# One row buffer for a two-pass channel-attention kernel: packed blocks read whole, other fills, fewer stores

## The chip, the core and the metric

The kernel runs on one core of a Trainium2 chip. The metric is the device time of one execution in microseconds (us). All tensors are bfloat16 in HBM; a "row" below means 768 bytes (384 channels) on each of the 128 partitions, 98,304 bytes in all.

## What is computed

The input `x` is 384 x 384 positions of 384 channels, 113.25 MB. Over all positions the mean and the maximum of each channel are taken, both go through the same small two-layer net, and a sigmoid gives one factor for each channel, by which the whole input is multiplied.

```python
xf = x.reshape(B, H * W, C)
gap = jnp.mean(xf, 1)
gmp = jnp.amax(xf, 1)
h_a = gap @ w1
h_a = h_a * (h_a > 0)
h_m = gmp @ w1
h_m = h_m * (h_m > 0)
scale = _sigmoid(h_a @ w2 + h_m @ w2)
return x * scale[:, None, None, :]
```

So every row must be read once before any row can be multiplied, and stored once after. What does not stay in the core's memory between the passes must be read a second time.

## The kernel before

The input is 1,152 rows, in blocks of some rows each (lines 112 to 123). A transfer moves n rows: on every partition one contiguous run of n x 768 bytes. All reads go on SP's queue, all stores on ACT's queue; both are first in, first out. The order of all instructions is written out by hand (`manual_schedule`, line 180), so each engine runs its work in the order in which the text issues it, and a read on SP's queue that waits for its buffer holds up all reads behind it.

**Memory.** `body` (line 149) has 264 rows: three slots of 31, 31 and 34 rows for reads that pass through, and from row 96 on seven homes of 24 rows. `held` (line 148) is another buffer of 21 rows. `acc` has 11 rows.

**First pass** (lines 220 to 386). A list `steps` of reads, tests, packs and one judgement is built and then issued. Each read is followed by its column sums on TensorE (`sums`, line 259) and its running maximum on VectorE (DVE) into `acc` (`maximum`, line 328, in pieces of at most 6 rows that alternate between the two halves of `acc`, `HALVES`). Some rows stay for the second pass:

- seven *packed blocks* of 32 rows. Three quarters (24 rows) are read into the block's home, the fourth ("part d", 8 rows) into one of two places in `held` (line 153). TensorE and ACT pack the 32 rows into the 24 of the home (`pack`, line 305), in two halves; ACT also tests whether the packing is without loss (`test`, line 295). The place of d is then free for the block after next.
- the last fills of the three slots (`STAYING`) and the last 21 rows, in `held` (`LAST_HELD`).
- ten rows copied into PSUM (line 383 and 385), and eight turned over into PSUM (`turn_over`, line 331) so that other rows can be refilled into their place (line 405).

Between the blocks, fills of up to 31 rows go round the three slots (`BETWEEN`, `PASSING`, `fill`, line 208). The last four reads are summed in another way (`tail_sums`, line 276), after the sums so far are turned (`turn_sums`, line 271). Before the last but one read's maxima `acc` is folded from 11 rows to 6 (`FOLD_BEFORE`, line 365).

**Between the passes** (lines 389 to 421). The two weight matrices are read, the refill of 8 rows and parts of `acc` as buffers are read, the maxima are folded, and the factors `scale_bc` come from ACT at line 421.

**Second pass** (lines 424 to 575). The rows that stayed are multiplied and stored, the 29 places of `PLACES` are read again (782 rows), multiplied and stored, and the packed blocks are unpacked in between (`unpack`, line 452), multiplied and stored by `finish` (line 484) and, for blocks 2 to 6, by the list `after` (line 500) in the last three turns. A place may be read as soon as its rows have left (`read`, line 509). At the end (line 576) stands a branch that reads the packed blocks again if a test failed; with this data it isn't taken.

Of the kernel before, what the change touches and what calls it, by code (L numbers as in the profile page):

```python
# [30 lines left out]
SLOT = 31  # L31
SLOTS = 3
RING = 96
G = 8
PACKED = 7
PSUM_ROWS = 8
# [3 lines left out]
HELD_ROWS = 21  # L40
# [4 lines left out]
FOLD_BEFORE = 2  # L45
BETWEEN = (
    (10, 31, 31, 31), (31, 31, 31), (31, 31, 31, 31), (31, 31, 31), (31, 31, 31, 31), (31, 31, 31), (30, 27),
)
PASSING = (25, 22, 21, 10, 17)
SHARED_FILL = 2  # L50
STAYING = {0: (16, 15), 1: (11, 10, 10), 2: (10, 9, 4, 6, 5)}
LAST_HELD = (6, 5, 4, 6)
# [7 lines left out]
FILLS = 16  # L60
# [5 lines left out]
HELD_STORES = (6, 7)  # L66
# [6 lines left out]
def kernel(  # L73
# [14 lines left out]
    NS = SLOTS  # L88
# [11 lines left out]
    consts = ctx.enter_context(tc.tile_pool(name="consts", bufs=1))  # L100
    xpool = ctx.enter_context(tc.tile_pool(name="xp", bufs=1))
# [511 lines left out]
```

## Time and profile before

| what | us |
|---|---|
| median of 3 runs | 728.07 (727.78 to 728.39) |
| the profiled execution, its own time | 727.18 |
| its span, first to last instruction | 725.4 |
| DVE busy in it | 565.1 |
| ACT busy in it | 349.6 |
| PE busy in it | 188.9 |

A profile is one execution. Its page shows busy times, the span in 40 slices of 18.1 us with the rate of the transfers in each, and the chain of waits that ended last. Views beside the page group busy time by stretches of the span, list instructions in order of time, list who waited for whom, and group instructions by their shape. Engines: PE = TensorE, PEld its weight loads, DVE = VectorE, ACT = ScalarE, SP = the queue of reads, ACTq = the queue of stores.

### The profile page before, as it was taken

How to read it: one execution, taken by the hardware profiler on the slowest of the kernel's cores; microseconds unless marked ns; L12 is line 12 of the kernel's file. 1: busy time of each engine (PE TensorE's matmuls, PEld its weight loads, DVE VectorE, ACT ScalarE, POOL GpSimd, SP SyncE). 2: the span in 40 equal slices, each digit the busy share in tenths (PEclk: the TensorE clock that was granted, in tenths of full speed). 3: DMA queues.
4: the chain of work that ended last, by engine and by line, in shares of the span. 5: the costliest groups of instructions: out<-in, count | busy, mean ns of one | idle time of the engine just before them, and what ended most of it. 6: DMA issues, size and time to landing. Idle time of an engine off the chain costs nothing.

```text
span 725.4 us, 3863 instructions
## 1 busy us (share of the span) xinstructions
PE 188.9 (26%) x1357; PEld 73.4 (10%) x1357; DVE 565.1 (78%) x438; ACT 349.6 (48%) x251; POOL 0.7 (0%) x6
## 2 busy tenths in 40 slices
PE   5756576876776561000000000000000000001000
PEld 1222222322222130000000000000000000001000
DVE  6899999989999998897966454798888889496200
ACT  6979999999999200057230022806254451200000
POOL 0000000000000000000000000000000000000000
PEclk9898977887988555555555555555555555555555
DMA  9999999999999988999999999999999999999998
GB/s 382 429 427 423 432 425 435 426 432 427 426 428 422 421 330 347 399 425 437 425 438 424 434 434 428 425 433 428 431 437 428 429 436 432 432 430 442 426 427 362
DMA packets 21843, 305.63 MB, mean 421 GB/s; under 512 B 2784, under 2 KB 3136, under 8 KB 8512
## 3 DMA queue, kind: packets, MB, share of 16 engines
q1 hardware_dynamic: 14048, 192.14, 62.4%
q10 hardware_dynamic: 7776, 113.25, 36.7%
q8 instruction: 10, 0.16, 0.1%
q14 instruction: 9, 0.07, 0.0%
HBM read 192.14 MB, written 113.25 MB: 421 GB/s over the span
## 4 chain that ended last, share of the span: by engine, by line
DMA 71%; DVE 20%; issue 2%; PE 0%; ACT 0%; SPq 0%; ACTq 0%; DVEq 0%
DMA body<-in_x_dram 52%; DMA out_dram<-body 19%; DVE acc L329 11%; DVE body L426 7%; DVE held L426 1%; DVE held L458 0%; DVE kept_ps L383 0%; DVE acc L426 0%; ACT held L477 0%; DVE acc L463 0%; DVE acc L370 0%; PE bank_a L263 0%; DVE body L458 0%; SPq L360 0%; PE bank_a L420 0%
## 5 line engine op out<-in xcount | busy, mean ns | idle before, releaser
L426 DVE TENSOR_TENSOR body<-body,scale_bc 128x9216 bf16<-128x9216 bf16 (+8 forms) x49 | 220.1, 4523 | 88.7 <-DMA body<-in_x_dram 87.5
L329 DVE TENSOR_TENSOR acc<-acc,body 128x2304 bf16<-128x2304 bf16 (+4 forms) x210 | 229.7, 1167 | 14.1 <-DMA body<-in_x_dram 14.1
L263 PE MATMUL bank_a<-body,small 128*1 128x512 bf16 (+2 forms) x849 | 91.8, 476 | 82.0 <-DMA body<-in_x_dram 82.0
L335 PE MATMUL words_ps<-ident_bf,acc 128*128 128x128 bf16 x24 | 2.7, 313 | 376.9 <-DVE acc L568 376.9
L291 ACT ACTIVATE held<-held 128x3072 uint8<-128x3072 uint8 (+1 forms) x35 | 82.0, 2344 | 1.1
L477 ACT COPY held<-body 128x1536 uint8<-128x1536 uint8 x8 | 11.8, 1474 | 141.6 <-DVE body L426 141.4
L290 ACT ACTIVATE held<-body,held 128x3072 uint8<-128x3072 int8 (+1 forms) x28 | 61.9, 2211 | 9.7 <-DMA body<-in_x_dram 9.2
L477 ACT COPY body<-body 128x1536 uint8<-128x1536 uint8 x20 | 29.5, 1476 | 63.3 <-DVE body L426 62.8
L477 ACT COPY body<-acc 128x1536 uint8<-128x1536 uint8 x34 | 49.5, 1473 | 8.0 <-DVE acc L463 7.6
L263 PEld LDWEIGHTS <-small 128*1 128x1 bf16 x891 | 30.2, 96 | 143.7 <-issue 123.3
L335 PEld LDWEIGHTS <-acc 128*128 128x128 bf16 x24 | 2.5, 147 | 377.3 <-DVE acc L568 377.3
L311 PE MATMUL words_ps<-body,scale_bc 128*128 128x512 fp8e4 (+1 forms) x126 | 39.6, 429 | 2.9 <-ACT body L318 2.9
L311 PE MATMUL words_ps<-body,w_sb 128*128 128x512 fp8e3 x84 | 27.1, 406 | 0.0
L311 PE MATMUL words_ps<-held,body 128*128 128x512 fp8e4 x84 | 25.5, 385 | 0.0
L317 ACT COPY body<-held 128x1536 uint8<-128x1536 uint8 x14 | 20.6, 1470 | 0.0
L477 ACT COPY acc<-body 128x1536 uint8<-128x1536 uint8 x14 | 20.5, 1466 | 0.0
L317 ACT COPY body<-body 128x1536 uint8<-128x1536 uint8 x14 | 20.4, 1461 | 0.0
L318 ACT ACTIVATE body<-words_ps 128x1536 uint16<-128x1536 f32 x14 | 20.1, 1439 | 0.0
L290 ACT ACTIVATE held<-held 128x3072 uint8<-128x3072 int8 x7 | 20.0, 2856 | 0.2
L329 DVE TENSOR_TENSOR acc<-acc,held 128x1920 bf16<-128x1920 bf16 (+4 forms) x18 | 17.5, 1012 | 0.1
L477 ACT COPY held<-acc 128x1536 uint8<-128x1536 uint8 x8 | 11.8, 1475 | 10.1 <-DVE acc L463 10.1
L458 DVE TENSOR_SCALAR held<-held 128x1536 uint16<-128x1536 uint16 x28 | 15.7, 560 | 1.0
(71 smaller groups left out, 173.4 us busy)
## 6 DMA issues: line engine op xcount, KB each, us to landing
body<-in_x_dram SPq DMA_DIRECT2D x20, 2976.0 KB, 21.7
body<-in_x_dram SPq DMA_DIRECT2D x16, 2880.0 KB, 25.0
out_dram<-body ACTq DMA_DIRECT2D x15, 2880.0 KB, 23.3
body<-in_x_dram SPq DMA_DIRECT2D x18, 2304.0 KB, 19.3
out_dram<-body ACTq DMA_DIRECT2D x16, 2304.0 KB, 21.8
out_dram<-body ACTq DMA_DIRECT2D x3, 4608.0 KB, 37.0
held<-in_x_dram SPq DMA_DIRECT2D x8, 768.0 KB, 22.4
body<-in_x_dram SPq DMA_DIRECT2D x5, 960.0 KB, 15.2
```

Source lines behind the costliest of these rows:

```text
L263: nc.tensor.matmul(sum_ps[q * QP:q * QP + 1, 0:g * P], lhsT=ones_bf[:, 0:1], rhs=rows[:, k:k + g, q * P:(q + 1) * P], start=(done + k == 0 ...
L290: nc.scalar.activation(out=out_, in_=rows, func=ACT.Square, bias=test_bias, scale=TEST_SCALE)
L291: nc.scalar.activation(out=out_, in_=out_, func=ACT.Square, bias=minus4, accum_out=tests[:, k:k + 1],)
L311: nc.tensor.matmul(words[:, c:c + BANK], lhsT=weights[2 * r + k], rhs=high(part(i, r), dt)[:, half * n + c:half * n + c + BANK], start=(r ...
L317: nc.scalar.copy(out=high(part(i, r), U8)[:, span], in_=low(part(i, r + 2), U8)[:, span])
L318: nc.scalar.activation(out=part(i, 2).rearrange("p n c -> p (n c)").bitcast(U16)[:, span], in_=words, func=ACT.Copy, bias=32767.5,)
L329: nc.vector.tensor_tensor(out=out_, in0=in0, in1=in1, op=ALU.max)
L335: nc.tensor.transpose(out=out_[:, r, q * P:(q + 1) * P], in_=rows[:, r, q * P:(q + 1) * P], identity=ident_bf)
L426: nc.vector.tensor_tensor(out=dst, in0=src, in1=scale_bc.unsqueeze(1).to_broadcast([P, n, C]), op=ALU.mult)
L458: nc.vector.tensor_scalar(out=u16(dst), in0=u16(src), scalar1=s1, scalar2=s2, op0=op0, op1=op1)
L477: nc.scalar.copy(out=dst, in_=src)
```

## The change

- `body` and `held` become one buffer `rows` of 285 rows: `held` is its first 5, `body` the 280 behind. The two places of d now lie inside `body` (`D_AT`), and the homes stand in another order (`HOME_AT`). In the source the rows of the packed blocks are ordered to fit (`FIRST_AT`, `FOURTH_AT`).
- Blocks 1, 2 and 3 are each read in one transfer of 32 rows, home and place of d together (`TOGETHER`). Blocks 0, 4, 5 and 6 are read in two parts as before (block 0 in three).
- Fills no longer go round three slots: each has its own place and size (`BETWEEN`, `PASSING` hold pairs of place and rows), and early ones also use homes that are not yet taken. The first has 21 rows where three reads of 8, 13 and 10 rows stood; the others between the blocks have 21 to 51.
- The second half of each packing is issued behind another fill (`PACK_BEHIND`); the judgement stands one slot later.
- The resident pieces of the slots are (16, 15), (11, 11, 9), (11, 10, 8, 5); the last four reads have 8, 2, 6 and 5 rows, and the eight rows that are turned over are the first of these.
- The packed blocks leave in five stores (two of 32 rows by `finish`, then 64, 48 and 48), where there were seven (48 and 16, then 48, 48, and 16, 24, 24). The ten rows kept in PSUM leave in one store instead of two, and the rows in `held` leave as 5 and 8.
- 24 instead of 16 small writes stand at DVE's start (`FILLS`).

```diff
@@ -28,28 +28,44 @@
-SLOT = 31
-SLOTS = 3
 RING = 96
 G = 8
 PACKED = 7
+HOME_AT = (96, 184, 128, 152, 256, 232, 208)
+D_AT = (120, 176)
+BODY_ROWS = 280
+FIRST_AT = (0, 104, 40, 64, 200, 176, 152)
+FOURTH_AT = (24, 96, 32, 88, 128, 136, 144)
+TOGETHER = (1, 2, 3)
+SLOTS = ((0, 31), (31, 31), (62, 34))
+SPARE = 93
 PSUM_ROWS = 8
 LATE_ROWS = 8
 BANK_ROWS = 2
 RING_BYTES = 256
-HELD_ROWS = 21
+HELD_ROWS = 5
 A = 11
 HALVES = ((0, 6), (6, 11))
 FIRST_LOAD = 4
 FOLD_BEFORE = 2
 BETWEEN = (
-    (10, 31, 31, 31), (31, 31, 31), (31, 31, 31, 31), (31, 31, 31), (31, 31, 31, 31), (31, 31, 31), (30, 27),
+    ((21, 30), (208, 48)), ((51, 21), (0, 49), (72, 21)), ((208, 51), (0, 46), (46, 34)),
+    ((208, 42), (0, 45), (45, 32)), ((208, 34), (0, 36), (36, 31), (67, 26)), ((0, 33), (33, 31), (64, 29)),
+    ((0, 25), (25, 23)),
 )
-PASSING = (25, 22, 21, 10, 17)
-SHARED_FILL = 2
-STAYING = {0: (16, 15), 1: (11, 10, 10), 2: (10, 9, 4, 6, 5)}
-LAST_HELD = (6, 5, 4, 6)
+PACK_BEHIND = (0, 2, 1, 1, 0, 0, 1)
+PASSING = ((62, 16), (78, 9), (0, 22), (31, 14), (45, 17))
+REFILL_AT = 62
+LAST_PASSING = (70, 17)
+STAYING = ((16, 15), (11, 11, 9), (11, 10, 8, 5))
+LAST_HELD = ((8,), (2, 6), (5,))
 PLACES = (
...
@@ -57,13 +73,12 @@
     + ((0, 30), (30, 30), (60, 30), (90, 30)) * 3 + ((0, 30), (30, 30), (60, 30), (90, 20))
 )
 FIRST_READ = (8, 16)
-FILLS = 16
+FILLS = 24
 OPENING = (0, 24, (3, 4))
 FIRST_PLACE = ((0, 8, (8, 8)), (0, 0, (8,)))
 SECOND_PLACE = ((1, 0, (8, 9)), (2, 0, (10,)))
 OTHER_PLACES = ((1, 17, (14,)), (2, 10, (24,)))
-HELD_STORES = (6, 7)
 TEST_SCALE = 0.031187
 SUM_TAIL = 4
 MM_ROWS = 4
...
@@ -109,16 +122,18 @@
         at += n
         return at - n, n
-    ps_block = take(PSUM_ROWS)
-    beside = take(BANK_ROWS + A)
+    for_psum = PSUM_ROWS + BANK_ROWS
+    first_block = take(for_psum + A)
     packed_block = take(GP * PACKED)
-    held_block = take(sum(LAST_HELD))
-    stay = {s: take(sum(pieces)) for s, pieces in STAYING.items()}
+    late_block, kept_block, held_block = (take(sum(pieces)) for pieces in LAST_HELD)
+    stay = [take(n) for _, n in SLOTS]
     refill = take(LATE_ROWS)
     passing_at, n_pass = at, TOT - at
-    between = [[take(n) for n in group] for group in BETWEEN]
-    passing = [take(n) for n in PASSING]
-    assert at == TOT and sum(n for _, n in PLACES) == n_pass and sum(LAST_HELD) == HELD_ROWS
+    between = [[take(n) for _, n in group] for group in BETWEEN]
+    passing = [take(n) for _, n in PASSING]
+    last_passing = take(LAST_PASSING[1])
+    assert at == TOT and sum(n for _, n in PLACES) == n_pass and held_block[1] == HELD_ROWS
+    assert late_block[1] == LATE_ROWS and kept_block[1] == G and [sum(p) for p in STAYING] == [n for _, n in SLOTS]
     at = passing_at
     again = [take(n) for _, n in PLACES]
...
@@ -145,14 +160,16 @@
     acc = consts.tile([P, A, C], BF16)
     nc.dynamic_dma_scratch_size = RING_BYTES
     nc.lookup_mloc("DynamicDMAScratchLoc").dims = [P, RING_BYTES]
-    held = nc.alloc_sbuf_tensor_at("held", [P, HELD_ROWS, C], BF16, offset=RING_BYTES).ap()
-    body = xpool.tile([P, RING + 3 * G * PACKED, C], BF16, name="body")
-    slots = [body[:, SLOT * i:SLOT * i + stay[i][1], :] for i in range(NS)]
-    spare = body[:, SLOT * NS, :]
-    homes = [body[:, RING + 3 * G * i:RING + 3 * G * (i + 1), :] for i in range(PACKED)]
-    fourth = [held[:, G * (i % 2):G * (i % 2 + 1), :] for i in range(PACKED)]
-    tested = held[:, 2 * G:2 * G + G // 2, :].rearrange("p n c -> p (n c)").bitcast(U8)
-    tests = held[:, 2 * G + G // 2, :].bitcast(F32)
+    rows = nc.alloc_sbuf_tensor_at("rows", [P, HELD_ROWS + BODY_ROWS, C], BF16, offset=RING_BYTES).ap()
+    held, body = rows[:, 0:HELD_ROWS, :], rows[:, HELD_ROWS:HELD_ROWS + BODY_ROWS, :]
+    slots = [body[:, lo:lo + n, :] for lo, n in SLOTS]
+    spare = body[:, SPARE, :]
+    homes = [body[:, lo:lo + 3 * G, :] for lo in HOME_AT]
+    d_places = [body[:, lo:lo + G, :] for lo in D_AT]
+    fourth = [d_places[i % 2] for i in range(PACKED)]
+    tested = held[:, 0:G // 2, :].rearrange("p n c -> p (n c)").bitcast(U8)
+    tests = held[:, G // 2, :].bitcast(F32)
     test_bias = tests[:, NT:NT + 1]
     minus4 = tests[:, NT + 1:NT + 2]
     test_sum = tests[:, NT + 2:NT + 3]
...
@@ -203,46 +220,40 @@
     steps = []
-    n_slot = 0
-    def fill(*parts):
-        nonlocal n_slot
+    def load(block, buf, pieces, lo=0):
         j = 0
-        for block, lo, hi in parts:
-            steps.append(("load", block, slots[n_slot % NS][:, j:j + hi - lo, :], lo, hi))
-            j += hi - lo
-            assert j <= SLOT
-        n_slot += 1
-    def whole(block):
-        return block, 0, block[1]
+        for m in pieces:
+            steps.append(("load", block, buf[:, j:j + m, :], lo + j, lo + j + m))
+            j += m
+    def fill(block, lo):
+        load(block, body[:, lo:lo + block[1], :], (block[1],))
     for i in range(PACKED):
-        first, d_at = 3 * G * i, 3 * G * PACKED + G * i
-        for lo, hi in ((0, FIRST_LOAD), (FIRST_LOAD, 3 * G)) if i == 0 else ((0, 3 * G),):
-            steps.append(("load", packed_block, homes[i][:, lo:hi, :], first + lo, first + hi))
-        steps.append(("load", packed_block, fourth[i], d_at, d_at + G))
+        if i in TOGETHER:
+            lo = min(HOME_AT[i], D_AT[i % 2])
+            load(packed_block, body[:, lo:lo + GP, :], (GP,), min(FIRST_AT[i], FOURTH_AT[i]))
+        else:
+            load(packed_block, homes[i], (FIRST_LOAD, 3 * G - FIRST_LOAD) if i == 0 else (3 * G,), FIRST_AT[i])
+            load(packed_block, fourth[i], (G,), FOURTH_AT[i])
         steps += [("test", i, 0), ("pack", i, 0), ("test", i, 1), ("test", i, 2)]
+        if i == 0:
+            fill(first_block, 0)
         for k, b in enumerate(between[i]):
-            if i == 0 and k == 0:
-                fill(whole(ps_block), whole(beside), whole(b))
-            else:
-                fill(whole(b))
-            if k == 1:
+            fill(b, BETWEEN[i][k][0])
+            if k == PACK_BEHIND[i]:
                 steps.append(("pack", i, 1))
-    for k, b in enumerate(passing[:-1]):
-        if k == SHARED_FILL:
-            fill(whole(b), whole(passing[k + 1]))
-        elif k != SHARED_FILL + 1:
-            fill(whole(b))
-    steps.append(("judge",))
-    fill(whole(refill), whole(passing[-1]))
-    assert n_slot % NS == next(iter(stay))
-    parts_left = [(stay[i], slots[i], pieces) for i, pieces in STAYING.items()] + [(held_block, held, LAST_HELD)]
-    for block, buf, pieces in parts_left:
-        for j, m in enumerate(pieces):
-            lo = sum(pieces[:j])
-            steps.append(("load", block, buf[:, lo:lo + m, :], lo, lo + m))
+    for k, b in enumerate(passing):
+        fill(b, PASSING[k][0])
+    fill(refill, REFILL_AT)
+    fill(last_passing, LAST_PASSING[0])
+    for k, pieces in enumerate(STAYING):
+        load(stay[k], slots[k], pieces)
+        if k == 0:
+            steps.append(("judge",))
+    for block, buf, pieces in zip((late_block, kept_block, held_block), (*d_places, held), LAST_HELD):
+        load(block, buf, pieces)
     loads = [st for st in steps if st[0] == "load"]
     tail_rows = sum(st[4] - st[3] for st in loads[len(loads) - SUM_TAIL:])
...
@@ -377,12 +388,11 @@
             e = min(e, c + m - j)
             maximum(acc[:, c:e, :], acc[:, c:e, :], rows[:, j:j + e - c, :])
             j += e - c
-        if block == held_block and lo < LATE_ROWS <= hi:
-            turn_over(late, held)
-        elif block == ps_block:
-            nc.vector.tensor_copy(out=kept_ps[:, 0:PSUM_ROWS, :].bitcast(U32), in_=rows.bitcast(U32))
-        elif block == beside:
-            nc.vector.tensor_copy(out=kept_b.bitcast(U32), in_=rows[:, 0:BANK_ROWS, :].bitcast(U32))
+        if block == late_block:
+            turn_over(late, rows)
+        elif block == first_block:
+            nc.vector.tensor_copy(out=kept_ps.bitcast(U32), in_=rows[:, 0:PSUM_ROWS, :].bitcast(U32))
+            nc.vector.tensor_copy(out=kept_b.bitcast(U32), in_=rows[:, PSUM_ROWS:for_psum, :].bitcast(U32))
         nth += 1
...
@@ -479,15 +489,16 @@
     def store(buf, block, lo):
         nc.scalar.dma_start(out=rows_of(orr, block)[:, lo:lo + buf.shape[1], :], in_=buf)
-    d_at = 3 * G * PACKED
+    def store_packed(lo, n, to):
+        store(body[:, lo:lo + n, :], packed_block, to)
     def finish(i):
         for rows in (homes[i], homes_d[i]):
             multiply(rows, rows)
         if i == 1:
-            store(body[:, RING:RING + 3 * G * 2, :], packed_block, 0)
-            store(held[:, 0:2 * G, :], packed_block, d_at)
+            store_packed(HOME_AT[0], GP, 0)
+            store_packed(D_AT[1], GP, FOURTH_AT[1])
     jobs = [[(unpack, 0, 0)], [(unpack, 0, 1)], [(unpack, 1, 0)], [(finish, 0)], [(unpack, 1, 1)], [], [(finish, 1)]]
...
@@ -497,14 +508,10 @@
     jobs.append([])
     jobs.append([(finish, PACKED - 1)])
-    after = [
-        [(body[:, RING + 3 * G * 2:RING + 3 * G * 4, :], 3 * G * 2)],
-        [(body[:, RING + 3 * G * 4:RING + 3 * G * 6, :], 3 * G * 4)],
-        [(held[:, 0:2 * G, :], d_at + 2 * G), (homes[1], d_at + 4 * G), (homes[6], 3 * G * 6)],
-    ]
+    after = [(D_AT[0], 2 * GP, FOURTH_AT[2]), (HOME_AT[5], 6 * G, FIRST_AT[5]), (HOME_AT[1], 6 * G, FOURTH_AT[4])]
     order = []
-    turn_of_row = [-1] * (RING + 3 * G * PACKED)
+    turn_of_row = [-1] * BODY_ROWS
     def read(last_turn, blocks_gone):
...
@@ -530,8 +537,9 @@
     put_slot(*OPENING)
     put_acc()
-    put(held_block, held[:, LATE_ROWS:, :], HELD_STORES, LATE_ROWS)
-    put(refill, held[:, 0:LATE_ROWS, :], (LATE_ROWS,))
+    put(held_block, held, (HELD_ROWS,))
+    put(kept_block, d_places[1], (G,))
+    put(refill, d_places[0], (LATE_ROWS,))
     for pieces in FIRST_PLACE:
         put_slot(*pieces)
     read(-1, 0)
```

More of the change, by code (lines that the diff above doesn't have):

```diff
@@ L87 @@
     TOT = HW // P
-    NS = SLOTS
     GP = 4 * G
@@ L98, in rows_of @@
         return ap[first * P:(first + n) * P, :].rearrange("(p n) c -> p n c", n=n)
-    consts = ctx.enter_context(tc.tile_pool(name="consts", bufs=1))
-    xpool = ctx.enter_context(tc.tile_pool(name="xp", bufs=1))
+    consts = ctx.enter_context(tc.tile_pool(name="consts", bufs=1, side="right"))
     psum = ctx.enter_context(tc.tile_pool(name="ps", bufs=1, space=bass.MemoryType.PSUM))
@@ L396, in acc_rows @@
     def acc_rows(ap, lo, hi):
-        return rows_of(ap, beside)[:, BANK_ROWS + lo:BANK_ROWS + hi, :]
+        return rows_of(ap, first_block)[:, for_psum + lo:for_psum + hi, :]
     acc_pieces = []
@@ L403, in load_acc @@
         acc_pieces.append((lo, hi))
-    nc.sync.dma_start(out=held[:, 0:LATE_ROWS, :], in_=rows_of(xr, refill))
+    nc.sync.dma_start(out=d_places[0], in_=rows_of(xr, refill))
     load_acc(folds[-1], A)
@@ L444 @@
     turns = len(PLACES)
-    homes_d = [held[:, G * (i % 2):G * (i % 2 + 1), :] for i in range(4)]
+    homes_d = [d_places[i % 2] for i in range(4)]
     homes_d += [homes[1][:, G * i:G * (i + 1), :] for i in range(3)]
@@ L448 @@
     HG = G // 2
-    m = held[:, 2 * G:2 * G + HG, :]
+    m = held[:, 0:HG, :]
     t = acc[:, G:G + HG // 2, :].rearrange("p n c -> p (n c)").bitcast(U8)
@@ L550 @@
     j = PLACES[-1][0] + PLACES[-1][1]
-    assert j + PSUM_ROWS + BANK_ROWS <= PLACES[-5][0] + PLACES[-5][1]
-    leaving = [(body[:, j:j + PSUM_ROWS, :], ps_block), (acc[:, 0:LATE_ROWS, :], held_block)]
-    leaving.append((body[:, j + PSUM_ROWS:j + PSUM_ROWS + BANK_ROWS, :], beside))
+    assert j + for_psum <= PLACES[-5][0] + PLACES[-5][1]
+    leaving = [(body[:, j:j + for_psum, :], first_block), (acc[:, 0:LATE_ROWS, :], late_block)]
     for turn in range(turns):
@@ L557 @@
         if turn >= turns - len(after):
-            for rows, lo in after[turn - turns + len(after)]:
-                store(rows, packed_block, lo)
+            store_packed(*after[turn - turns])
         store(buf, b, 0)
@@ L569 @@
             turn_over(late, to)
-            multiply(leaving[0][0], kept_ps[:, 0:PSUM_ROWS, :])
-            multiply(leaving[2][0], kept_b)
+            multiply(leaving[0][0][:, 0:PSUM_ROWS, :], kept_ps)
+            multiply(leaving[0][0][:, PSUM_ROWS:, :], kept_b)
             multiply(to, late)
@@ L577 @@
         for i in range(PACKED):
-            for buf, lo in ((homes[i], 3 * G * i), (homes_d[i], d_at + G * i)):
+            for buf, lo in ((homes[i], FIRST_AT[i]), (homes_d[i], FOURTH_AT[i])):
                 n = buf.shape[1]
```

## The prediction

> **What bounds the kernel now.** I read the page first: which resource is busy in every slice, and where its row dips.
>
> ```profile
> span 725.4 us, 3863 instructions
> ...
> DVE  6899999989999998897966454798888889496200
> ...
> DMA  9999999999999988999999999999999999999998
> GB/s 382 429 427 423 432 425 435 426 432 427 426 428 422 421 330 347 399 425 437 425 438 424 434 434 428 425 433 428 431 437 428 429 436 432 432 430 442 426 427 362
> DMA packets 21843, 305.63 MB, mean 421 GB/s; under 512 B 2784, under 2 KB 3136, under 8 KB 8512
> ...
> DMA 71%; DVE 20%; issue 2%; PE 0%; ACT 0%; SPq 0%; ACTq 0%; DVEq 0%
> ```
>
> The transfers run at 420 to 440 GB/s in every slice but the first, three in the middle and the last. So the kernel is bound by moving 305.63 MB, and only three things can shorten it: fewer bytes, a higher rate, smaller holes. The next view, busy time by stretch, puts numbers on rate and hole. Its columns are PE, weight loads, DVE, ACT, POOL, clock, DMA share, GB/s.
>
> ```profile
> core 0: us, PE busy (x) PEld busy (x) DVE busy (x) ACT busy (x) POOL busy (x), PEclk, DMA share, GB/s
> 0.00:4.00 4.00, 0.00 (x0) 0.00 (x1) 1.84 (x25) 2.38 (x7) 0.70 (x6) 1.00 0.61 214
> 40.00:44.00 4.00, 3.43 (x24) 1.07 (x24) 3.74 (x4) 1.04 (x1) 0.00 (x0) 0.57 0.98 415
> 60.00:232.00 172.00, 124.91 (x852) 46.15 (x852) 163.11 (x152) 170.13 (x113) 0.00 (x0) 0.83 1.00 428
> 246.00:264.00 18.00, 10.22 (x72) 2.83 (x72) 18.00 (x17) 0.00 (x0) 0.00 (x0) 0.50 1.01 415
> 266.00:282.00 16.00, 7.87 (x111) 6.88 (x105) 13.86 (x18) 1.78 (x7) 0.00 (x0) 0.61 0.66 240
> 300.00:680.00 380.00, 2.74 (x24) 2.48 (x24) 287.76 (x161) 121.03 (x84) 0.00 (x0) 0.50 1.01 431
> ```
>
> Inside both passes the rate is flat (428 and 431 GB/s). The hole is 266 to 282 us: 16 x (1 - 240/428) = 7.0 us are lost there, between the last read of the first pass and a steady flow of stores. What ends the hole is seen in the timeline (start, length, engine, line, and the wait before it) and in the list of waits:
>
> ```profile
> 238.93 0.22 ACT L324 ACTIVATE held<-held 128x35 f32<-128x35 f32 x1
> ...
> 243.10 24.37 DVE L329 TENSOR_TENSOR acc<-acc,body 128x2304 bf16<-128x2304 bf16 x22 [0.42 <-DMA body<-in_x_dram]
> ...
> 252.82 7.36 SPq L360 DMA_DIRECT2D held<-in_x_dram  x4
> ...
> 267.38 2.43 DVE L329 TENSOR_TENSOR acc<-acc,held 128x2304 bf16<-128x2304 bf16 x2
> ...
> 269.27 2.48 PEld L335 LDWEIGHTS <-held 128*128 128x128 bf16 x24
> ...
> 272.04 0.34 SPq L405 DMA_DIRECT2D held<-in_x_dram  x1
> ...
> 277.68 1.63 DVE L426 TENSOR_TENSOR body<-body,scale_bc 128x1152 bf16<-128x1152 bf16 x2 [1.17 <-ACT scale_bc L421]
> 278.47 1.21 ACTq L435 DMA_DIRECT2D out_dram<-body  x2
> ```
>
> ```profile
> DVE acc L329 <- DMA body<-in_x_dram: 14.1, 22, 1.9
> ```
>
> From 243.10 the DVE never waits again before the scale: it is fully busy for 18 of 18 us in 246:264 and is behind the reads at their end. The landing at 243.1 is the 17-row load of the last passing fill. The first store, at 278.47, is therefore set by that landing plus the DVE's remaining maxima, not by the last read. The DVE waits 14.1 us for reads in the whole first pass, so before 243 it keeps pace and has a little room.
>
> **The change part by part.** A row is 768 bytes on 128 partitions, 98,304 bytes, which is 0.2297 us at 428 GB/s.
>
> Bytes: the first pass reads 1,152 rows before and after, the second pass rereads the same 782 + 19 rows, all 1,152 are stored. Nothing is saved: 0.
>
> Number of transfers: counted in the two texts. First-pass reads go from 60 to 53: block reads 15 to 12 (three of them come whole), fills 31 to 28, resident pieces 10 to 9, last ones 4 to 4. Stores go from 54 to 51: packed ones 7 to 5, closing ones 3 to 2. The price of one comes from the two read rates. In 246:264 the queue carries pieces of about 9 rows: 415 x 18 = 7.47 MB, 76 rows, some 8.4 transfers, where the steady state with 5 transfers per 125 rows would have had 3.0. The time lost is 18 x (1 - 415/428) = 0.55 us over 5.4 extra transfers, 0.10 us each. That is an upper end, since nothing says that all of the loss is a transfer's own cost; the lower end is 0. I take 0.10, because the flow is saturated in both stretches (share 1.00 and 1.01) and nothing else there differs so plainly.
>
> Where it counts: ahead of the 17-row landing there are 46 transfers before and 40 after, for the same 1,035 rows. The landing comes 6 x 0.10 = 0.6 us earlier. The seventh read lies behind that landing, in the stretch that the DVE sets: worth nothing. The three stores all lie behind the hole, on a flow that the queue sets: 0.3 us.
>
> The DVE's work behind the landing: 134 rows (17, 96 resident, 21 last) in both. Following the two halves of the accumulator through the piece sizes gives 27 maxima and folds before and 29 after.
>
> ```profile
> L329 DVE TENSOR_TENSOR acc<-acc,body 128x2304 bf16<-128x2304 bf16 x6 | 8.1, 1357 | 0.4 <-DMA body<-in_x_dram 0.4
> ...
> L329 DVE TENSOR_TENSOR acc<-acc 128x384 bf16<-128x384 bf16 x2 | 0.7, 358 | 0.1
> ```
>
> In these groups by form, six rows take 1357 ns and one row 358, so a row is 200 ns and an instruction's own part 158. In the run at 243.10, 24.37 us for 22 operations over 96 + 17 rows leave (24.37 - 113 x 0.2)/22 = 0.08 us each, as they overlap. Two more cost 0.16 us (up to 0.32 if they did not overlap). The first store thus comes 0.6 - 0.16 = 0.44 us earlier.
>
> Refill inside the hole: the last four loads become 8, 2, 6, 5 instead of 6, 5, 4, 6, and the eight rows that are turned over now arrive first. Before, the turning (24 at 269.27) follows 11 rows of tail sums, after it 8, so the refill at 272.04 leaves some 0.5 us earlier. Worth 0: the refill and the accumulator pieces behind it have 6 us until the store at 278.47 and fill only a part of them.
>
> Early fills of 21 to 51 rows: they put more rows behind one wait. The DVE takes 31 rows in 6.71 us (the chain of waits, below), 0.2165 us per row, the queue 0.2297.
>
> ```profile
> 97.46 6.71 DVE acc L329 x6
> ```
>
> Working the queue against the DVE, with a load handed over only when whole: the 48-row read makes the DVE idle 48 x 0.2297 - 30 x 0.2165 = 4.5 us, the 49-row one 1.5, the 51-row one 1.8, the first 45-row one 1.1. With some 1.3 for the first fill that is 10.2 us, of the 14.1 that it waits now. So the DVE is back at the queue's pace well before the 17-row landing. Cost 0; with the room gone each further microsecond would move the first store by one.
>
> Whole blocks: the read of block 2 or 3 now waits for the packing of block 0 or 1 with all its 32 rows, where only eight waited, and all later fills stand behind it on SP's queue. ACT is through with block 0 at 41 us (1.04 us busy in 40:44, the row is above). The queue wants block 2 after 254 rows, 58 us. Cover 17 us; cost 0. Between the blocks stand 99, 91, 131, 119, 127 and 93 rows of fills instead of 124 and 93 in turn, so ACT's packing stays spread. It judges at 238.93, and the reads into its scratch rows are issued from 252.82 on (both in the timeline above): 14 us of cover there.
>
> Eight more fill writes at the start: 25 writes take 1.84 us in 0:4, so 0.6 us more on the DVE. The list of waits is exact there:
>
> ```profile
> DVE acc L370 <- DMA body<-in_x_dram: 4.3, 1, 4.3
> ```
>
> It waits 4.3 us for the 20-row load anyway: cost 0. Without that cover it would be 0.6.
>
> Second pass: the same reads of 24 and 30 rows in the same places, multiplications and unpacking as before. The first packed store is 32 + 32 rows instead of 48 + 16, and the last ones are 64, 48 and 48 instead of 48, 48 and 16 + 24 + 24; DVE work ends long before the stores do (0 in the last two slices), so what counts is only the number of transfers.
>
> Sum: 0.44 + 0.3 = 0.74 us less, against the profiled run's own time of 727.18 us (span 725.4 and 1.8 around it), so 726.4 for that run. It lies 0.9 us under the median shown, 728.07; carried over, 727.3 us. By the bounds of the two prices the gain is between -0.3 (transfers free, two maxima at full price) and 1.0, so 727.0 to 728.4.
>
> **The rivals.** *Faster than that.* The second pass runs at 431 GB/s with pieces of 24 to 48 rows. If large pieces themselves carry that rate into the first pass, its 264 us shrink by 264 x 3/431 = 1.8 us, with the stores 2.1: 726.0. For it: the first twelve fills average 37 rows. Against: the second pass also mixes reads and stores, which may be the cause, and the later half of the first pass goes back to 23 to 36 rows, the last third to 9 to 25.
>
> *Nothing.* The transfers' own cost is hidden between the sixteen engines and the hole stays as it is: 728.1. For it: the DMA share is 1.00 in both stretches.
>
> *Slower: the queue runs dry.* Place: the 22-row read, the first that goes into rows just freed from the 25-row fill. It waits for those maxima with only 23 + 16 + 9 rows (11.0 us) in front of it. The DVE starts them about 1.2 us late (24 + 8 block rows just before take it 6.9 us, the 25 rows land in 5.7) and takes 5.4, and a read needs about 1 us to its first byte: 3.4 us in hand. The 14-row read behind it has the same. If the large fills leave the DVE later than 3.4 us there, every further microsecond is lost to the queue, and again at the first store; 2.5 us late gives 728.07 - 0.74 + 2.5 = 729.8. For it: the reads wait for the DVE already.
>
> ```profile
> SPq L360 <- DVE acc L329: 211.6, 34, 14.1
> ```
>
> Against: that wait is what a full queue looks like, and the four long DVE waits all lie in the first 130 us.
>
> [...]
>
> **How the numbers follow.** Forecast 0.43 (727.3), faster rival 0.28 (726.0), nothing 0.10 (728.1), dry queue 0.15 (729.8), fetches 0.04 (728.5). A difference under 0.2%, 1.46 us, can hardly be told from no change here: the bounds are 726.6 and 729.5. The faster rival falls under the first in nearly all its weight, the forecast with a tenth: 0.32. Above the second lie most of the dry queue and a little of the rest: 0.16. The rest, 0.52, is between. The range runs from 725.5, just under the faster rival, to 729.5, which leaves out the worse half of the dry queue; the forecast's own range is 727.0 to 728.4.
>
> **What would show it.** In the profile after: 140 transfers where there were 150; the 17-row landing near 242.5; no wait of the DVE for a read from there to the scale; the refill near 271.5; the first store near 278.0; DMA at 428 in 60:232 (431 speaks for the faster rival, a dip near 215 to 230 for the dry queue); long DVE waits at the 48-, 49-, 51- and 45-row reads only. I am wrong if the DVE has waits behind the 17-row landing, if the hole grows past 7.0 us, or if the rate in the second pass changes.

## The result, and the profile after

The changed kernel takes 725.75 us (median of 7 runs, 725.41 to 726.02) where the kernel before took 728.39 on the same chip (7 runs, 727.48 to 728.98): a ratio of 0.9966, with a 95% interval of 0.9954 to 0.9977, or 2.6 us less. Measured again (the ninth experiment) the changed kernel takes 725.75, against 727.69 beside it: 0.9977 [0.9967, 0.9987]. Over both, a gain of 1.9 to 2.6 us. The profiled execution of after has a time of 725.41 and a span of 723.6.

The page of after, the rows of resource and rate in 40 slices, the packets and the chain:

```profile
span 723.6 us, 3882 instructions
...
DMA  9999999999999979999999999999999999999997
GB/s 380 434 438 435 417 442 427 429 430 432 431 426 428 426 312 356 400 433 431 433 431 431 434 428 431 434 430 435 430 429 432 437 432 430 430 433 439 442 426 339
DMA packets 20403, 305.63 MB, mean 422 GB/s; under 512 B 2624, under 2 KB 2976, under 8 KB 7200
...
DMA 63%; DVE 25%; issue 3%; PE 2%; ACT 1%; SPq 0%; DVEq 0%; ACTq 0%
```

The bytes are the same (305.63 MB), the transfers still fill every slice but those of the hole, and the packets fell by 21,843 - 20,403 = 1,440. The third experiment adds 28 transfers and 4,032 packets, 144 for each, so 1,440 packets are the ten transfers that were counted. What changed lies in the slices of the first pass, ahead of the hole. Busy time by stretch, with the prediction's columns (rate last):

```profile
60.00:232.00 172.00, 121.92 (x882) 46.89 (x879) 167.59 (x156) 165.62 (x111) 0.00 (x0) 0.84 1.00 431
246.00:264.00 18.00, 10.71 (x79) 2.91 (x73) 18.00 (x17) 0.00 (x0) 0.00 (x0) 0.50 1.01 424
266.00:282.00 16.00, 6.41 (x100) 5.69 (x99) 13.75 (x18) 0.83 (x3) 0.00 (x0) 0.50 0.67 235
300.00:680.00 380.00, 2.74 (x24) 2.47 (x24) 286.25 (x161) 121.03 (x84) 0.00 (x0) 0.50 1.01 432
```

The first pass went from 428 to 431 GB/s, which is 172 x (1 - 428/431) = 1.2 us in that stretch alone, and the end of the pass from 415 to 424. The second pass stayed (431 before, 432 after). The hole, worked as in the prediction, costs 16 x (1 - 235/431) = 7.3 us in the same window, where it was 7.0; in a window moved along with the first store (264.5:280.5, 229 GB/s) it costs 7.5. The timeline (start, length, engine, line, and the wait before it) gives the same in times:

```profile
241.56 26.48 DVE L340 TENSOR_TENSOR acc<-acc,rows 128x1920 bf16<-128x1920 bf16 x26 [0.87 <-DMA rows<-in_x_dram]
268.07 1.16 DVE L340 TENSOR_TENSOR acc<-acc 128x1920 bf16<-128x1920 bf16 x1
...
269.74 0.34 SPq L415 DMA_DIRECT2D rows<-in_x_dram  x1
...
276.20 1.63 DVE L436 TENSOR_TENSOR rows<-rows,scale_bc 128x1152 bf16<-128x1152 bf16 x2 [1.17 <-ACT scale_bc L431]
277.00 1.21 ACTq L445 DMA_DIRECT2D out_dram<-rows  x2
```

The 17-row landing comes at 241.56 where it came at 243.10, 1.54 us earlier; the first store at 277.00 instead of 278.47, 1.47 earlier. Of the 1.8 us between the spans 1.5 are there before the first store. The list of waits (total, times, longest) and the DVE's timeline show the early fills:

```profile
DVE acc L340 <- DMA rows<-in_x_dram: 13.6, 8, 5.6
```

```profile
15.57 4.57 DVE L340 TENSOR_TENSOR acc<-acc,rows 128x1920 bf16<-128x1920 bf16 x4 [1.23 <-DMA rows<-in_x_dram]
...
34.49 21.60 DVE L340 TENSOR_TENSOR acc<-acc,rows 128x1920 bf16<-128x1920 bf16 x19 [5.64 <-DMA rows<-in_x_dram]
...
57.59 21.79 DVE L340 TENSOR_TENSOR acc<-acc,rows 128x2304 bf16<-128x2304 bf16 x19 [1.51 <-DMA rows<-in_x_dram]
...
81.20 43.99 DVE L340 TENSOR_TENSOR acc<-acc,rows 128x1920 bf16<-128x1920 bf16 x40 [1.81 <-DMA rows<-in_x_dram]
...
126.31 57.40 DVE L340 TENSOR_TENSOR acc<-acc,rows 128x1920 bf16<-128x1920 bf16 x54 [1.11 <-DMA rows<-in_x_dram]
184.84 42.44 DVE L340 TENSOR_TENSOR acc<-acc,rows 128x1920 bf16<-128x1920 bf16 x40 [1.13 <-DMA rows<-in_x_dram]
```

Eight waits instead of 22, with almost the same sum (13.6 us against 14.1): the first fill (1.23), the 48-, 49-, 51- and 45-row reads (5.64, 1.51, 1.81 and 1.11), the 33-row read (1.13) and two short ones. There is none from 241.56 to the scale.

So the reads of the first pass became faster by more than six transfers at 0.10 us could make them. One part of the diff is in neither the list of the change nor the sum, the placing of the buffers (its first lines stand in a piece of the diff that is left out above):

```diff
-    consts = ctx.enter_context(tc.tile_pool(name="consts", bufs=1))
-    xpool = ctx.enter_context(tc.tile_pool(name="xp", bufs=1))
+    consts = ctx.enter_context(tc.tile_pool(name="consts", bufs=1, side="right"))
...
-    body = xpool.tile([P, RING + 3 * G * PACKED, C], BF16, name="body")
+    rows = nc.alloc_sbuf_tensor_at("rows", [P, HELD_ROWS + BODY_ROWS, C], BF16, offset=RING_BYTES).ap()
```

Before, `held` stood at byte 256 of each partition, the constants behind it, and `body`, which most reads go into, behind those at byte 26,592. That is a multiple of 32, not of 64. With the constants moved to the other end, `rows` starts at 256. A row has 768 = 3 x 256 bytes, so each read into `rows` starts at a multiple of 256, and each read into the old `body` 224 bytes past one. The trace keeps the time of every piece, that is of one partition's run of a transfer. Medians of the reads between 40 and 232 us, in ns, and the share of pieces that lie more than 1.5 and more than 6 ns above 8.2 + 28.25 a row, the line on which the unhindered ones lie:

```
kernel   start of the buffer      8 rows  24 rows  31 rows  32 rows  >1.5 ns  >6 ns
before   26,592 (224 past)          234*    689      887       -       .69     .21
after    256    (0)                 234     686      884      912      .00     .00
* these go into `held`, at 256; without them the shares of before are .82 and .25
```

Two theories were tried on the chip. By the first the *place* makes the gain: reads whose pieces start off a multiple of 256 bytes take longer. By the second, that of the faster rival and of the prediction's sum, it is the *transfers*: larger and fewer of them.

### The profile page after: what moved, and what is told of

Its sections match the earlier page's. It is cut to its first block, busy times and chain, and to the rows that moved or that the text cites. A ratio compares the mean times of both kernels' runs of the same rounds, so it can differ in the third digit from the quotient of the medians.

```text
span 723.6 us, 3882 instructions
## 1 busy us (share of the span) xinstructions
PE 184.7 (26%) x1363; PEld 74.2 (10%) x1363; DVE 564.1 (78%) x445; ACT 349.8 (48%) x251; POOL 0.7 (0%) x6
## 2 busy tenths in 40 slices
DMA packets 20403, 305.63 MB, mean 422 GB/s; under 512 B 2624, under 2 KB 2976, under 8 KB 7200
## 4 chain that ended last, share of the span: by engine, by line
DMA 63%; DVE 25%; issue 3%; PE 2%; ACT 1%; SPq 0%; DVEq 0%; ACTq 0%
DMA rows<-in_x_dram 40%; DMA out_dram<-rows 23%; DVE acc L340 16%; DVE rows L436 9%; PE words_ps L322 1%; ACT rows L328 0%; DVE acc L436 0%; SPq L371 0%; PE bank_a L274 0%; ACT rows L329 0%; ACT rows L487 0%; PE bank_a L430 0%; ACT scale_bc L431 0%; DVE small L424 0%; PE bank_a L423 0%
## 5 line engine op out<-in xcount | busy, mean ns | idle before, releaser
L436 DVE TENSOR_TENSOR rows<-rows,scale_bc 128x9216 bf16<-128x9216 bf16 (+9 forms) x56 | 230.9, 4164 | 91.2 <-DMA rows<-in_x_dram 90.0
L340 DVE TENSOR_TENSOR acc<-acc,rows 128x2304 bf16<-128x2304 bf16 (+4 forms) x227 | 245.0, 1154 | 13.9 <-DMA rows<-in_x_dram 13.6
L487 ACT COPY rows<-rows 128x1536 uint8<-128x1536 uint8 x28 | 41.3, 1476 | 204.2 <-DVE rows L436 144.8
L274 PE MATMUL bank_a<-rows,small 128*1 128x512 bf16 (+3 forms) x897 | 93.3, 466 | 80.9 <-DMA rows<-in_x_dram 76.1
L301 ACT ACTIVATE rows<-rows 128x3072 uint8<-128x3072 int8 (+1 forms) x35 | 81.9, 2341 | 9.1 <-DMA rows<-in_x_dram 8.4
L302 ACT ACTIVATE rows<-rows 128x3072 uint8<-128x3072 uint8 (+1 forms) x35 | 82.0, 2344 | 1.1
L487 ACT COPY rows<-acc 128x1536 uint8<-128x1536 uint8 x42 | 60.5, 1473 | 18.2 <-DVE acc L473 17.7
L322 PE MATMUL words_ps<-rows,scale_bc 128*128 128x512 fp8e4 (+1 forms) x126 | 37.9, 414 | 9.2 <-ACT rows L329 9.2
L328 ACT COPY rows<-rows 128x1536 uint8<-128x1536 uint8 x28 | 39.7, 1468 | 0.4 <-PE words_ps L322 0.4
L322 PE MATMUL words_ps<-rows 128*128 128x512 fp8e3 (+1 forms) x126 | 35.8, 394 | 0.0
L468 DVE TENSOR_SCALAR rows<-rows 128x1536 uint16<-128x1536 uint16 x56 | 31.3, 560 | 1.9
```

The source lines that it names most:

```text
L274: nc.tensor.matmul(sum_ps[q * QP:q * QP + 1, 0:g * P], lhsT=ones_bf[:, 0:1], rhs=rows[:, k:k + g, q * P:(q + 1) * P], start=(done + k == 0 ...
L301: nc.scalar.activation(out=out_, in_=rows, func=ACT.Square, bias=test_bias, scale=TEST_SCALE)
L302: nc.scalar.activation(out=out_, in_=out_, func=ACT.Square, bias=minus4, accum_out=tests[:, k:k + 1],)
L322: nc.tensor.matmul(words[:, c:c + BANK], lhsT=weights[2 * r + k], rhs=high(part(i, r), dt)[:, half * n + c:half * n + c + BANK], start=(r ...
L328: nc.scalar.copy(out=high(part(i, r), U8)[:, span], in_=low(part(i, r + 2), U8)[:, span])
L340: nc.vector.tensor_tensor(out=out_, in0=in0, in1=in1, op=ALU.max)
```

## The experiments

Each is shown with its edit, what was expected, and the median beside that of the kernel before on the same chip.

### The kernel before, constants at the other end

```diff
-    consts = ctx.enter_context(tc.tile_pool(name="consts", bufs=1))
+    consts = ctx.enter_context(tc.tile_pool(name="consts", bufs=1, side="right"))
```

> The kernel before with one edit: the small constants lie behind the big buffer instead of ahead of it, so body starts at byte 16,512 of a partition (a multiple of 128) instead of 26,592 (a multiple of 32 only). No transfer, piece or instruction changes. Theory A (place): in the first pass of before, the reads into body take 887 or 894 ns for 31 rows where after, whose buffer starts at 256, takes 884; a place that is not a multiple of 64 costs a read 3 to 10 ns for each piece when reads alone fill the queue. Then the 31-row pieces come down to 884, the 17-row landing from 243.1 to about 241.8, the rate in 60:232 from 428 to 431 GB/s, and the time by 1.2 to 1.8 us. Theory B (larger fills and fewer transfers do it all): no change, 0 +- 0.5 us, pieces stay at 887.

727.05 us against 727.56: 0.9997 [0.9988, 1.0006], no gain that can be told. `body` now starts at 16,512, a multiple of 128 but not of 256. The share of slow pieces fell only from .69 to .43 (over 6 ns: .21 to .16), the landing comes at 242.81 and the first store at 278.26, 0.3 and 0.2 us earlier. So being moved is not enough, nor is a multiple of 128, and the first theory, as it was put here with a multiple of 64, falls.

### The changed kernel, its buffer 32 bytes on

```diff
-    rows = nc.alloc_sbuf_tensor_at("rows", [P, HELD_ROWS + BODY_ROWS, C], BF16, offset=RING_BYTES).ap()
+    rows = nc.alloc_sbuf_tensor_at("rows", [P, HELD_ROWS + BODY_ROWS, C], BF16, offset=RING_BYTES + 32).ap()
```

> The changed kernel with its one buffer 32 bytes further on, at 288 instead of 256. Theory A: its first-pass pieces grow by 3 to 10 ns each, as before had them (31 rows 884 to about 888), and the time rises by 1.0 to 1.8 us. Theory B: no change, 0 +- 0.5 us.

727.43 against 727.56: 1.0005 [0.9996, 1.0014]. The whole gain is gone, with every fill, whole block and store of the change in place. Stretches and the first store of this kernel:

```profile
60.00:232.00 172.00, 121.54 (x876) 46.47 (x871) 167.06 (x155) 165.03 (x111) 0.00 (x0) 0.86 1.01 428
246.00:264.00 18.00, 10.02 (x70) 2.88 (x70) 18.00 (x18) 0.00 (x0) 0.00 (x0) 0.50 1.01 416
...
300.00:680.00 380.00, 2.74 (x24) 2.48 (x24) 286.28 (x161) 121.02 (x84) 0.00 (x0) 0.50 1.01 432
```

```profile
278.87 1.21 ACTq L445 DMA_DIRECT2D out_dram<-rows  x2
```

428 and 416 GB/s are the rates of before, and the first store is back behind 278. The second pass still runs at 432: no loss shows in its rate. Fills of 21 to 51 rows alone bring no higher rate.

### The changed kernel, second-pass reads in halves

```diff
-        for m in FIRST_READ if k == 0 else (n,):
+        for m in FIRST_READ if k == 0 else (n // 2, n - n // 2):
```

> The changed kernel, but each of the 28 later places of the second pass is read in two halves: 28 more transfers for the same bytes, in a stretch that the queue alone bounds. It measures the price of a transfer, which the prediction took as 0.10 us with bounds 0 and 0.10. At 0.10 the time rises by 2.8 us. If the six transfers saved ahead of the 17-row landing were worth the 1.5 us by which it came earlier, the price is 0.25 and the time rises by 7 us. If transfers are free, 0.

731.65 against 727.56: 1.0058 [1.0045, 1.0072], and 5.9 us over the changed kernel, 0.21 for each of the 28 more transfers. The packets and the stretch of the second pass:

```profile
DMA packets 24435, 305.63 MB, mean 419 GB/s; under 512 B 3072, under 2 KB 3424, under 8 KB 7904
```

```profile
300.00:680.00 380.00, 2.74 (x24) 2.47 (x24) 275.54 (x159) 120.92 (x84) 0.00 (x0) 0.50 1.01 428
```

428 instead of 432 GB/s is 380 x (1 - 428/432) = 3.5 us, 0.13 each. The rest is at the end: the trace's last sixteen 4-byte pieces on the queue of stores (each store has sixteen: 816 for the 51 of after) end between 723.2 and 727.9 us in this kernel and between 719.9 and 721.3 in after. 0.21 is therefore an upper end for the second pass, and holds for reads only: whether a store that is saved brings as much it doesn't show.

### The changed kernel with 16 writes at the DVE's start

```diff
-FILLS = 24
+FILLS = 16
```

> The changed kernel with 16 instead of 24 small writes at DVE's start. The prediction costs them at nothing, under the wait for the first reads: 0 +- 0.4 us. [...]

725.91 against 727.56: 0.9982 [0.9968, 0.9996]. First store at 276.98 (277.00 in after). The eight writes cost nothing.

### The kernel before, its buffer at 16,384

```diff
-    consts = ctx.enter_context(tc.tile_pool(name="consts", bufs=1))
-    xpool = ctx.enter_context(tc.tile_pool(name="xp", bufs=1))
+    consts = ctx.enter_context(tc.tile_pool(name="consts", bufs=1, side="right"))
...
-    body = xpool.tile([P, RING + 3 * G * PACKED, C], BF16, name="body")
+    body = nc.alloc_sbuf_tensor_at("body", [P, RING + 3 * G * PACKED, C], BF16, offset=16384).ap()
```

> The kernel before with its constants behind and body at byte 16,384, a multiple of 256 (e1 had 16,512, a multiple of 128, and its 31-row pieces stayed about 3 ns over those of the changed kernel). Theory A, mended: what counts is a multiple of 256. Then the 31-row pieces come to 884 ns, 60:232 runs at 431 GB/s, the first store comes near 277.0 and the time falls by 1.2 to 1.8 us against before, to within 0.5 us of the changed kernel: the placing alone is nearly the whole gain. Theory B: fills and fewer transfers give most of it; then this one gains 0.5 us at most, as e1 did.

725.37 against 727.72: 0.9973 [0.9963, 0.9984]. This is the old program in every transfer, fill and store; only the place differs, by 128 bytes from that of the first experiment. Its stretches, and its timeline at the 17-row landing and the first store:

```profile
60.00:232.00 172.00, 122.25 (x852) 45.73 (x852) 164.46 (x153) 170.54 (x113) 0.00 (x0) 0.85 1.00 431
246.00:264.00 18.00, 10.73 (x78) 2.91 (x75) 18.00 (x18) 0.00 (x0) 0.00 (x0) 0.50 1.01 422
...
300.00:680.00 380.00, 2.74 (x24) 2.48 (x24) 286.40 (x161) 121.04 (x84) 0.00 (x0) 0.50 1.01 432
```

```profile
241.78 24.25 DVE L328 TENSOR_TENSOR acc<-acc,body 128x2304 bf16<-128x2304 bf16 x22 [0.54 <-DMA body<-in_x_dram]
...
277.13 1.21 ACTq L434 DMA_DIRECT2D out_dram<-body  x2
```

431 GB/s with fills of at most 31 rows, the landing 1.32 us and the first store 1.34 us earlier than before. With the second experiment this is the whole table of place and program: old program misplaced 727.6, old program placed 725.4, new program misplaced 727.4, new program placed 725.75. The place is worth 1.9 to 2.4 us in the old program (this experiment and the tenth) and 1.4 to 1.7 in the new one (second, sixth and eleventh), and the rest of the change, within some 0.4 us, nothing. Of the 2.0 us between the spans of before and of this kernel (725.4 and 723.4), 1.34 stand at the first store. The other 0.66 lie behind it, where the placed kernels differ among each other by as much (446.3 to 447.1 us from the first store to the end), so that no cause is shown for them.

### The changed kernel, its buffer 128 bytes on

```diff
-offset=RING_BYTES).ap()
+offset=RING_BYTES + 128).ap()
```

> The changed kernel with its buffer 128 bytes further on, at 384. Theory A, mended: pieces 3 ns longer (as in e1), without the 10 ns ones of the 32-byte offset; the time rises by 0.7 to 1.4 us against the changed kernel. If a multiple of 64 or 128 is enough: 0.

727.12 against 727.72: 0.9995 [0.9982, 1.0007]. The timeline:

```profile
242.87 26.56 DVE L340 TENSOR_TENSOR acc<-acc,rows 128x1920 bf16<-128x1920 bf16 x26 [1.07 <-DMA rows<-in_x_dram]
...
278.39 1.21 ACTq L445 DMA_DIRECT2D out_dram<-rows  x2
```

1.3 and 1.4 us later than in after, from 128 bytes. The start 128 bytes on cost 1.4 us of the time (727.12 against 725.75), the one 32 bytes on 1.7 (727.43, second experiment).

### The changed kernel, its fills between the blocks in halves

```diff
-            fill(b, BETWEEN[i][k][0])
+            lo, n = BETWEEN[i][k]
+            load(b, body[:, lo:lo + n, :], (n // 2, n - n // 2))
```

> The changed kernel with each of the 20 fills between the packed blocks read in two halves into the same place: pieces of 10 to 26 rows, 20 more transfers, the same bytes. Price of a transfer 0.10: the 17-row landing and the first store come 2.0 us later, time +2.0 us. Price 0.21 (as e3 showed where stores share the queue): +4.2 us. If it is the size of the early fills that gains, more than that; if neither, 0.

726.54 against 727.72: 0.9983 [0.9971, 0.9994]; 20 transfers more, all ahead of the 17-row landing, in a queue that carries reads alone. Stretch and timeline:

```profile
60.00:232.00 172.00, 125.45 (x876) 47.29 (x873) 162.95 (x159) 164.94 (x111) 0.00 (x0) 0.81 1.01 430
```

```profile
242.37 26.48 DVE L341 TENSOR_TENSOR acc<-acc,rows 128x1920 bf16<-128x1920 bf16 x26 [0.18 <-DMA rows<-in_x_dram]
...
277.70 1.21 ACTq L446 DMA_DIRECT2D out_dram<-rows  x2
```

The landing comes 242.37 - 241.56 = 0.81 us later than in after, the first store 0.70, the time is 0.8 longer: 0.04 us for each transfer. Fills of 10 to 26 rows run at 430 GB/s when they are well placed.

### The changed kernel, no block in one read

```diff
-TOGETHER = (1, 2, 3)
+TOGETHER = ()
```

> The changed kernel with blocks 1, 2 and 3 read in two parts again, 24 and 8 rows: 3 more transfers ahead of the 17-row landing. Price 0.10: +0.3 us; 0.21: +0.6 us. A rival by which reading home and d in one run matters by itself: +1 us or more.

725.22 against 727.72: 0.9967 [0.9956, 0.9979], first store at 276.95. The three whole blocks bring nothing that can be measured; three transfers at 0.04 would be 0.12.

### The changed kernel once more, and the kernel before at 16,384 once more, on one chip

No edit: the kernels of the result and of the fifth experiment, side by side.

> The changed kernel itself, beside the next run on the same chip: what do fills, whole blocks, tail pieces and fewer stores give once the placing is the same? Theory A (placing is all): equal to before-at-256 within 0.5 us. Theory B (the rest gives some of it): 0.7 us or more faster than it, as the prediction's sum of 0.74 us said.

> The kernel before with body at byte 16,384 again: 0.2 to 0.3% faster than before, as in e5, and within 0.5 us of the changed kernel beside it by theory A; 0.7 us or more slower than that by theory B.

725.75 and 725.83 against 727.69: 0.9977 [0.9967, 0.9987] and 0.9976 [0.9966, 0.9986]. The old program, placed, and the new one take the same time.

### The changed kernel, its buffer 64 bytes on

```diff
-offset=RING_BYTES).ap()
+offset=RING_BYTES + 64).ap()
```

> The changed kernel 64 bytes further on, at 320. By theory A any place that is not a multiple of 256 costs the pieces 3 ns or more; by how many multiples of 32 it is off the pieces with 10 ns were a quarter (32 off) or few (128 off). Slower than the changed kernel by 1.0 to 1.7 us; if 64 were enough, 0.

727.13 against 727.69: 0.9994 [0.9985, 1.0003]; landing at 242.72, first store at 278.26. Of the starts that were tried, 256 and 16,384 are fast, and those 32, 64, 128 and 224 past a multiple of 256 are all slow.

None of these kernels is better than the changed one beyond the intervals: the placed old program (725.4 and 725.8) and the one without whole blocks (725.2) equal it.

## Why the prediction was right or wrong

**The placing, which has no term in the sum.** This is the step that failed: behind "Nothing is saved: 0" for the bytes only transfers, operations and stores were priced. The pool's side and the fixed start of `rows` were in the diff, and no sentence asked what an address could cost. The runs put nearly the whole gain there: 1.32 of the 1.54 us at the 17-row landing, 1.34 of the 1.47 us at the first store (fifth experiment against before). By the pieces it is much the same size: summed over the reads from 30 to 266 us and divided by sixteen engines, the time above the line is 1.9 us in before, 0.3 in the placed old program and 0.3 in after. That the time fell into the stated range was therefore luck: the range reached down to 725.5 for the sake of the faster rival, and nearly all of the gain came from neither that rival's cause nor the sum's.

**The price of a transfer, 0.10 us: too high by more than two.** It was worked out from 415 against 428 GB/s in 246:264, since "nothing else there differs so plainly". Something else did: the misplaced pieces. Their loss went by the piece and not by the byte (in the second experiment the median is 4 ns longer at 9 rows and at 51), so it should weigh most where pieces are small. Placing alone lifts that stretch from 415 to 422 (fifth experiment), and the same working with 422 and 431 would have given 18 x (1 - 422/431) / 5.4 = 0.07. Halving the fills, with 20 transfers more, measured 0.04. So the six transfers ahead of the landing are worth 0.24, not 0.6; after and the placed old program lie 0.22 apart there (241.56, 241.78). The forecast's own range was also a little too wide at its fast end: with 0.10 for a transfer and nothing for the two operations its terms give 0.6 + 0.3 = 0.9 us, not 1.0.

**Two more DVE operations: 0.16 forecast.** From the landing to the first store after takes 35.44 us and the placed old program 35.35: 0.09. That is right in sign and about half in size, and of the forecast's 0.44 for the first store 0.13 remain (277.13 to 277.00).

**Three stores, 0.3: not seen.** From the first store to the span's end there are 446.9 us before, 446.6 in after and 446.3 in the placed old program, which has all the old stores. What a store is worth wasn't tried by itself.

**The costs of nothing held.** This goes for the whole blocks (eighth experiment), the eight writes (fourth) and the early fills: the long DVE waits stand where the working put them (5.64, 1.51, 1.81 and 1.11 us, forecast 4.5, 1.5, 1.8 and 1.1), the DVE is back in time, and no wait follows the 17-row landing. The mark "only" there was missed: the DVE also waits 1.13 us for the 33-row read at 184.84. The refill leaves at 269.74, 2.3 us earlier, 1.5 of it with the landing and 0.8 behind it (forecast 0.5); that this brought nothing is argued from its cover, not tried.

**The bound held.** The kernel is still bound by its transfers (431 and 432 GB/s inside the passes at a share of 1.00 and 1.01, and 63% of the chain), and the first store follows the 17-row landing plus the DVE's remaining maxima in every kernel here whose timeline shows that landing (35.3 to 35.5 us behind it). One sign of being wrong did come: the hole grew past 7.0 us, to 7.3 in the same window and 7.5 in one moved along. It belongs to neither the rewrite nor the place, since 266:282 runs at 230 GB/s in the first experiment and 227 in the second, both misplaced and with their first store near 278.5, against 240 in before. So the 7.0 was one profile's figure; why it is smaller there stays open.

**The rivals.** The faster one gave nearly the time (726.0) and its mark came (431 in 60:232), but its mechanism falls: the second experiment has the large pieces at 428, the fifth the small ones at 431. A mark that two causes leave alike doesn't choose between them. *Nothing* holds for the rewrite by itself, once the place is the same, but not for the change, which moved the buffer too. The dry queue left no sign: the DVE's waits behind 216 us are 0.29 and 0.87, and the rate shows no dip there (430 GB/s in 215:230, 425 before). Its 1 us from a read's issue to the first byte is what the traces have where nothing is ahead of it in the queue: 1.01 us for the first read of before (0.74 to 1.75), 0.98 for the refill of after (269.74 to 270.72). The 0.04 for fetches (728.5) rests on no row: no run shows a fetch that waited. The ten 16 KB pieces on queue q8, which the pages call instruction, take 0.9 to 1.3 us each in after and 1.0 to 1.3 in before; when each was asked for, and for which engine, the traces don't show. The time lies in the range given but below the forecast's own (727.0 to 728.4). The gain, 0.34% with an interval from 0.23%, is larger than the 0.2% within which the likeliest case had put it; in the ninth experiment it is 0.23% with an interval from 0.13%, which leaves that open.

## What to carry to other kernels

Ahead of any tuning of transfer sizes, look up the byte at which each large buffer starts: here a start at a multiple of 256 was worth all that the whole rewrite brought (1.9 to 2.4 us in the old program), and it took a few edited lines. A price taken from a slow stretch belongs to all that is different in that stretch, so ask what else is small, late or misplaced there before it is put into a sum. Read a diff for what it moves in memory too, since a buffer that goes or a pool that changes sides shifts the addresses behind it, as here `body` went from byte 26,592 to 16,512 with the constants moved (first experiment).

## What the runs showed of the hardware

**Reads whose pieces started off a multiple of 256 bytes in the core's memory took longer in the first pass.** Medians and shares as in the table above:

```
kernel             start past a multiple of 256   24 rows  31 rows  >1.5 ns  >6 ns  lost us
before             224                              689      887      .69     .21    1.9
before, moved      128                              689      885      .43     .16    1.5
before, at 16,384    0                              686      884      .00     .00    0.3
after                0                              686      884      .00     .00    0.3
after + 32          32                              689      887      .93     .26    2.1
after + 64          64                              688      886      .82     .26    1.8
after + 128        128                              689      886      .64     .24    1.7
```

The last column is the time above the line, summed over the reads from 30 to 266 us and divided by sixteen. The shares of the first three kernels count the 8-row pieces that go into `held` and are well placed, those of the others have none such.

The median misplaced piece takes 1 to 3 ns more, and one in six to one in four loses 6 to 12 ns. The two starts that are a multiple of 32 but not of 64 lost most: of the pieces of nine rows and more between 40 and 266 us, 743 of 4,689 lie over 10 ns above the line in before and 772 of 4,590 at 32 past, but 137 to 213 of some 4,600 at 64 and 128 past, and 11 in after. Of the starts that were tried, 0 past a multiple of 256 has 0.3 us above the line, and 32, 64, 128 and 224 past it have 1.5 to 2.1. The cause the runs don't show; how far past doesn't order the loss, as 32 past has as much as 224 past (2.1 and 1.9 us).

**Little or nothing of it was left in the second pass, where reads and stores run at once.** There the median 24-row piece that is read takes 686 ns and the median 30-row piece 855 in every kernel of the table, misplaced or not, and the rate in 300:680 is 431 to 432 GB/s in all of them. Among the pieces stored between 285 and 690 us, however, 7 to 10% lie more than 1.5 ns above the line in the misplaced kernels and 2 to 3% in the two placed ones of the table, so a loss of some tenths of a us isn't excluded.

**One more transfer cost little:** 0.04 us among the reads of the first pass (seventh experiment), at most 0.21 among the reads and stores of the second (third).

What stays open: why only some misplaced pieces lose 6 to 12 ns, and by what the second pass hides the loss of its reads. Neither was tried.
